# Linear attention with a cosine layer and soft experts: key maxima by VectorE and DRAM, token softmax on 128 columns

## The chip, the cores and the metric

The kernel runs on one core of one Trainium2 chip. The metric is the device time of one execution in microseconds. Engines are named as the profile names them: PE (TensorE), DVE (VectorE), ACT (ScalarE), POOL (GpSimd), SP (SyncE, which issues the DMAs).

## What is computed

```python
# q, k, v: 8 batches, 8 heads, 576 tokens, 64 wide
k_s = softmax(k, axis=tokens); q_s = softmax(q, axis=width)
x = q_s @ (k_s.T @ v)               # per batch and head; then 4608 tokens x 512
h = x @ w_in                         # 512 -> 2048
x = (h * cos(h)) @ w_out             # 2048 -> 512
logits = x @ phi                     # 32 slots: 8 experts of 4
d = softmax(logits, axis=tokens)     # over all 4608 tokens
slot_out = experts(d.T @ x)          # relu(s @ w1[e]) @ w2[e]
out = softmax(logits, axis=slots) @ slot_out
```

All inputs are float32 but for w_in and w_out, which come as 64-bit words and are narrowed on the chip.

## The kernel before

The tokens go through in ten parts: parts 0 to 7 have 512 tokens, parts 8 and 9 have 256. A part has 16 steps (one per 128 rows of the 2048-wide layer): `mm1` (line 917, twelve matmuls into a buffer of tag h, of which there are three), `round_u`, `frac`, `cosine` and `gate` (lines 922 to 941, on DVE and ACT), which make g = h cos h. Since only x @ phi and d.T @ x are needed of the second layer, phi is folded into w_out: `logits` (line 943) multiplies g by the folded wphi, several steps at a time (list NTL says after which steps), and `g_tr` (line 962) then transposes g in place on DVE in blocks of 32.

When a part's logits are complete (a 128x128 tile, 32 slots by four row groups of 128 tokens), `p1` copies them to LTs. `p2(d, 0)` spreads them with the constant rc to all row groups as 128 x 512 in PSUM (line 983). `p3` takes the running maximum, `p4` the exponent and sum, `p5` a block transposition into ee. `g_mm` (line 1035) accumulates ee.T @ g over tokens with 32 x 32 tiles, and `g_add` adds that to a total that `ac` rescales. `p2(d, 1)` and `c1` to `c3` make the slot softmax.

Keys are handled a batch ahead: `k_max` (line 632) reduces over the tokens that lie in one partition, `k_tr` transposes on PE (line 654), `k_diag` reduces (661) and multiplies with the identity (666), `k_bc` sums with ones to broadcast the maxima to all partitions (675), `k_bc_ev` copies them to km on ACT (681). Then `k_sub`, `k_exp`, `k_v`, `k_fin`. Queries: `q_max`, `q_sub`, `q_exp`, `q_sum`, `q_rec`, `q_mul`, transposition `q_tr` with its copy, `q_kv`, and the split of x into two halves `x_hi`, `x_lo`, from which `mm1` reads.

The order of the instructions on each engine is fixed when the kernel is built. `Issue` (line 257) is a list planner: each `op` has an engine, a cost, its predecessors and a due time from the table PLACES["AT"]; PLACES["ENG"] gives the engine where there is a choice (P is GpSimd, D VectorE, A ScalarE). Each engine then runs its queue strictly in order. PSUM buffers are counted in rings: four of tag m for everything around the main matmuls, three of tag h for `mm1`. All DMAs are issued by SP, also in order.

After the last part comes a tail: the totals are folded (`e_fold`), the expert weights (w_u, in units of 1 MB whose loads are released by buffers that come free) are multiplied in `e_si`, `e_w1`, `e_w2`, and `e_mm` writes the output. Where PE would stand, filler matmuls (`keep_warm`, line 1553) are queued.

## Time and profile before

| | before |
|---|---|
| time, median of 3 runs | 710.34 us (707.34 to 710.55) |
| the profiled execution, its own time | 714.83 us |
| its span, first to last instruction | 712.4 us |
| PE busy | 671.6 us, 94% |
| DVE busy | 566.7 us, 80% |
| ACT busy | 370.7 us, 52% |
| POOL busy | 117.2 us, 16% |
| PE's granted clock, mean | 0.967 |

A row of time gives the start from the beginning of the span, a duration, engine, line of the kernel, operation, output and inputs, shape and count. Records of pipelined matmuls overlap, so the distance from one start to the next tells what a matmul costs. A float32 matmul leaves two records.

### The profile page before, as it was taken

What the parts mean: (1) busy time and instruction counts of PE and PEld (TensorE: products, weight loads), DVE (VectorE), ACT (ScalarE), POOL (GpSimd) and SP (SyncE); (2) the same over time, 40 slices, a digit from 0 to 9 for tenths busy, and PEclk for the clock granted to TensorE, in tenths of its full rate; (3) what the DMA queues carried; (4) which work ended last, traced back from release to release, by engine and by line L of the source; (5) the groups of instructions that cost most, each with busy time, mean ns of one, the idle gap of its engine ahead of it and who ended that gap; (6) DMA issues with size and microseconds to landing.
All of it is one profiled execution on the core that took longest, in us unless ns stands there. A gap on an engine that the chain in (4) does not pass through costs nothing.

```text
span 712.4 us, 16382 instructions
## 1 busy us (share of the span) xinstructions
PE 671.6 (94%) x6901; PEld 494.4 (69%) x6901; DVE 566.7 (80%) x1077; ACT 370.7 (52%) x618; POOL 117.2 (16%) x116
## 2 busy tenths in 40 slices
PE   7599899999999999999999899999999999999991
PEld 5467676777777777787787578768778888853330
DVE  6779899898999999989998997886886887732142
ACT  2868887484465374477285745523553535410041
POOL 1433641320030150240232111000000000000000
PEclk9779899999999999999999999999999999999996
...
DMA packets 53032, 97.58 MB, mean 137 GB/s; under 512 B 7776, under 2 KB 33376, under 8 KB 47712
## 3 DMA queue, kind: packets, MB, share of 16 engines
...
q14 instruction: 18, 0.15, 0.1%
...
## 4 chain that ended last, share of the span: by engine, by line
PE 74%; DVE 11%; DMA 8%; ACT 2%; issue 1%; POOL 1%; SPq 1%; DVEq 0%; ACTq 0%; POOLq 0%
PE ps_h L917 48%; PE ps_m L1035 5%; PE ps_LT L957 4%; PE ps_LT L1553 3%; DMA w_u<-in_moe_w_dram 3%; PE ps_m L707 2%; DMA Q<-in_q_dram 2%; PE ps_m L566 2%; PE ps_m L607 2%; DMA KVB<-in_k_dram 2%; DVE T L933 2%; DVE G L964 1%; DMA out_dram<-ob 1%; PE ps_h L1224 1%; DVE G L941 1%
## 5 line engine op out<-in xcount | busy, mean ns | idle before, releaser
L917 PE MATMUL ps_h<-XH,W 128*128 128x512 f32 x1024 | 334.2, 399 | 1.0 <-DVE G L941 0.9
L917 PEld LDWEIGHTS ps_h<-XH,W 128*128 128x128 f32 x1024 | 192.8, 188 | 56.0 <-issue 10.5
L917 PE MATMUL ps_h<-XL,W 128*128 128x512 f32 x512 | 201.3, 393 | 0.0
L938 ACT ACTIVATE T<-T 128x512 f32<-128x512 f32 (+1 forms) x160 | 93.6, 590 | 139.8 <-DVE T L933 139.5
L941 DVE TENSOR_TENSOR G<-T,ps_h 128x512 f32<-128x512 f32 (+1 forms) x160 | 99.3, 627 | 24.7 <-ACT T L938 18.3
L933 DVE SCALAR_TENSOR_TENSOR T<-T,ps_h 128x512 f32<-128x512 int32 (+1 forms) x160 | 100.2, 628 | 16.8 <-ACT T L925 13.8
L917 PEld LDWEIGHTS ps_h<-XL,W 128*128 128x128 f32 x512 | 96.5, 189 | 20.1 <-DVE XL L630 0.4
L925 ACT ACTIVATE T<-ps_h,quarter 128x512 int32<-128x512 f32 (+1 forms) x107 | 68.7, 644 | 79.6 <-PE ps_h L917 78.2
L964 DVE STREAM_TRANSPOSE G<-G 128x512 f32<-128x512 f32 (+1 forms) x160 | 96.8, 636 | 0.8 <-PE ps_LT L957 0.8
L553 POOL TENSOR_TENSOR B<-Q,qm 128x512 f32<-128x512 f32 x23 | 26.4, 1155 | 200.4 <-PE ps_m L566 68.9
L917 PEld LDWEIGHTS ps_h<-xe,W 128*128 128x128 f32 x384 | 46.7, 188 | 2.7 <-DVE G L941 1.0
L917 PE MATMUL ps_h<-xe,W 128*128 128x256 f32 x384 | 48.5, 284 | 0.0
L1035 PE MATMUL ps_m<-G,A 32*32 32x512 f32 x1152 | 42.7, 620 | 0.9 <-DVE G L964 0.9
L531 POOL TENSOR_TENSOR Q<-Q,qm 128x512 f32<-128x512 f32 x26 | 28.2, 1089 | 89.1 <-DVE qm L528 87.0
L957 PE MATMUL ps_LT<-G,wphi 128*32 128x128 f32 x1152 | 39.3, 276 | 1.5 <-DVE G L941 1.4
L684 POOL TENSOR_TENSOR KVB<-KVB,km 128x576 f32<-128x576 f32 x24 | 35.9, 1525 | 18.6 <-ACT km L681 18.6
L957 PEld LDWEIGHTS ps_LT<-G,wphi 128*32 128x32 f32 x1152 | 29.4, 109 | 12.4 <-issue 9.0
L927 DVE TENSOR_SCALAR T<-ps_h 128x512 int32<-128x512 f32 (+1 forms) x53 | 33.3, 628 | 5.3 <-PE ps_h L917 5.2
L1553 PE MATMUL ps_LT<-ones 128*128 128x512 f32 x109 | 32.3, 442 | 2.1 <-DVE r L448 2.1
L938 ACT ACT_TABLE_LOAD x25 | 32.1, 1283 | 0.4
L1035 PEld LDWEIGHTS ps_m<-G,A 32*32 32x32 f32 x1152 | 19.5, 105 | 17.2 <-issue 9.2
L1553 PEld LDWEIGHTS ps_LT<-ones 128*128 128x128 f32 x109 | 21.8, 210 | 13.6 <-issue 7.4
...
## 6 DMA issues: line engine op xcount, KB each, us to landing
...
```

The source lines that it names most:

```text
L531: (nc.vector if eng == "DVE" else nc.gpsimd).tensor_tensor(out=qv(t), in0=qv(t), in1=qm[:, t].unsqueeze(2).to_broadcast([128, 8, 64]), op= ...
L684: (nc.vector if eng == "DVE" else nc.gpsimd).tensor_tensor(out=k_t[:, t], in0=k_t[:, t], in1=km[:, t].unsqueeze(1).to_broadcast([128, KC, ...
L917: nc.tensor.matmul(out=u_t[s], lhsT=w[:, wi, kk, o:o + 128], rhs=x[xi][:, kk], start=(kk == 0 and n == 0), stop=(kk == 3 and n == 2),)
L925: nc.scalar.activation(out=t.bitcast(I32), in_=u_t[s], func=ACTF.Identity, bias=quarter)
L927: nc.vector.tensor_scalar(out=t.bitcast(I32), in0=u_t[s], scalar1=0.25, scalar2=None, op0=ALU.add)
L933: nc.vector.scalar_tensor_tensor(out=t, in0=t.bitcast(I32), scalar=0.25, in1=u_t[s], op0=ALU.subtract, op1=ALU.subtract)
L938: nc.scalar.activation(out=t_t[s], in_=t_t[s], func=ACTF.Sin, scale=-UNDER_TWO_PI)
L941: nc.vector.tensor_tensor(out=g_of(s), in0=t_t.pop(s), in1=u_t.pop(s), op=ALU.mult)
L957: nc.tensor.matmul(out=lt_t[d][o:o + 32, 0:128], lhsT=w2sb[:, f], rhs=g[:, 128 * c:128 * c + 128], start=(f0 < m), stop=(f0 >= NF - m),)
L964: nc.vector.transpose(out=g_of(s), in_=g_of(s))
L1035: nc.tensor.matmul(out=st["gp"][i][32 * c:32 * c + 32].rearrange("p (f b) -> p f b", f=NF), lhsT=ee[o, 32 * j:32 * j + 32], rhs=gs(d)[o, : ...
L1553: nc.tensor.matmul(out=warm[when], lhsT=ones_r, rhs=ones_r.unsqueeze(1).to_broadcast([128, 4, 128]), start=True, stop=True,)
```

## The change

Three things change in what is computed where, and the planner's tables are new for nearly all operations.

- Token softmax of parts 0 to 7: `p2(d, 0)` is gone. The maximum, the exponent and the sum are taken on LTs itself, 128 columns, with a running maximum for each row group and slot. After a block transposition of 128 columns, `copies` spreads the result to all row groups by four matmuls of 32 rows with rr, one for each row group, into four buffers of tag m, and `take_copy` brings them to ee, on ACT or DVE. Before part 8, which works as before, `merge` brings the four row groups to one maximum.
- Keys of batches 2 to 7 (KROW): in place of `k_tr`, `k_diag`, `k_bc` and the copy there is `k_row`: DVE transposes km in blocks of 32 and reduces, a DMA writes the 128 x 8 maxima to DRAM, two DMAs read them back to 64 partitions each, and DVE takes the maximum of two halves into km.
- Loads: the first key loads are issued ahead of the first query loads.

Beside these, rr is made with the constants, `e_sel` stands earlier in the list, and part 0 takes its logits every two steps, part 9 in five groups in place of two. The diff without the due times and without the other engine strings:

```diff
...
-        "k_sub": "PPDDDPPPPDPDDPPPPPPPPDPPPPPPPPDP",
-        "q_sub": "PDDPPPPPPDPPPPPDDDDPPPPPPPDPPPPDPPDP",
-        "q_mul": "PDDPPDPPPPPPPDDPPDPDDPPPPDPDDPPPDPPD",
...
+        "k_sub": "DDPPPPPPPPPPPPPPPPDPPPDPDDPPPPPP",
+        "q_sub": "PDDPPPPPPPPPPPPPDPPPPPPPDPPDPPPPPPDD",
+        "q_mul": "DDDPPPPDDPPPPPPDPPPPPPPDPPDDPDDPPPPP",
...
+        "tc": "DAADAAADDDAAAADADAADDDADDADDAAAD",
...
-    "NTL": [[3, 7, 11, 15], [3, 7, 11, 15], [7, 15]],
+    "NTL": [[1, 3, 5, 7, 9, 11, 13, 15], [3, 7, 11, 15], [3, 7, 11, 13, 15]],
...
+    "KROW": 2,
...
         nc.vector.tensor_add(r32, r32, ident[:, 96:128])
+        nc.vector.tensor_copy(rr, r32.unsqueeze(1).to_broadcast([128, 4, 32]))
...
 
     km = sbt([128, 4, 64], "km1")
-    kmx = sbt([128, 4], "kmx")
+    kmx = sbt([128, 8], "kmx")
...
     def k_bc_ev():
         nc.scalar.copy(out=km.rearrange("p t d -> p (t d)"), in_=pm_t.pop("kb")[:, 0:256])
+    dram = ctx.enter_context(tc.tile_pool(name="dk", bufs=1, space=bass.MemoryType.DRAM))
+    kd = dram.tile([4, 256], F32, name="kd")
+    def k_row(part):
+        m = abuf[:, 3]
+        if part == 0:
+            nc.vector.transpose(out=m[:, 0:256], in_=km.rearrange("p t d -> p (t d)"))
+            nc.vector.reduce_max(
+                out=kmx, in_=m[:, 0:256].rearrange("p (j r) -> p j r", r=32), axis=AX.X
+            )
+        elif part == 1:
+            nc.sync.dma_start(out=kd.rearrange("g (e j) -> (g e) j", j=8), in_=kmx)
+        elif part == 2:
+            for h in range(2):
+                nc.sync.dma_start(
+                    out=m[64 * h:64 * h + 64],
+                    in_=kd[2 * h:2 * h + 2].rearrange("a f -> (a f)").partition_broadcast(64),
+                )
+        else:
+            nc.vector.tensor_tensor(
+                out=km.rearrange("p t d -> p (t d)").rearrange("p (j e) -> p j e", j=8),
+                in0=m[:, 0:256].rearrange("p (e j) -> p j e", j=8),
+                in1=m[:, 256:512].rearrange("p (e j) -> p j e", j=8), op=ALU.max,
+            )
     def k_sub(t, eng):
         (nc.vector if eng == "DVE" else nc.gpsimd).tensor_tensor(
...
     def p3(d):
-        nc.vector.reduce_max(out=es, in_=st["r"][:, 0:parts[d][2]], axis=AX.X)
+        if d < 8:
+            nc.vector.reduce_max(out=es, in_=st["lt"], axis=AX.X)
+        else:
+            nc.vector.reduce_max(out=es, in_=st["r"][:, 0:parts[d][2]], axis=AX.X)
         if d == 0:
             nc.vector.tensor_scalar(
                 out=nmx[0], in0=es, scalar1=-1.0, scalar2=None, op0=ALU.mult
             )
         else:
             nc.vector.scalar_tensor_tensor(
-                out=nmx[d % 2], in0=es, scalar=-1.0, in1=nmx[1 - d % 2], op0=ALU.mult, op1=ALU.min
+                out=nmx[d % 2], in0=es, scalar=-1.0,
+                in1=st.pop("nm")[:, 32:33] if d == 8 else nmx[1 - d % 2], op0=ALU.mult, op1=ALU.min
             )
     def p4(d):
-        nt = parts[d][2]
+        nt = 128 if d < 8 else parts[d][2]
         if d:
             nc.scalar.activation(
                 out=ac, in_=nmx[1 - d % 2], func=ACTF.Exp, scale=-1.0, bias=nmx[d % 2]
             )
         nc.scalar.activation(
-            out=eT[:, 0:nt], in_=st.pop("r")[:, 0:nt], func=ACTF.Exp, bias=nmx[d % 2],
-            accum_out=es if d else esacc,
+            out=eT[:, 0:nt], in_=st["lt"] if d < 8 else st.pop("r")[:, 0:nt], func=ACTF.Exp,
+            bias=nmx[d % 2], accum_out=es if d else esacc,
         )
     def p5(d):
-        nt = parts[d][2]
-        nc.vector.transpose(out=ee[:, 0:nt], in_=eT[:, 0:nt])
+        if d < 8:
+            nc.vector.transpose(out=eT[:, 128:256], in_=eT[:, 0:128])
+        else:
+            nt = parts[d][2]
+            nc.vector.transpose(out=ee[:, 0:nt], in_=eT[:, 0:nt])
+    def copies(d):
+        st["ex"] = [misc() for c in range(4)]
+        for c in range(4):
+            o = slice(32 * c, 32 * c + 32)
+            nc.tensor.matmul(
+                out=st["ex"][c][:, 0:128], lhsT=rr[o].rearrange("p r s -> p (r s)"),
+                rhs=eT[o, 128:256], start=True, stop=True, tile_position=(32 * c, 0),
+            )
+    def take_copy(d, c, eng):
+        (nc.vector.tensor_copy if eng == "DVE" else nc.scalar.copy)(
+            out=ee[:, 128 * c:128 * c + 128], in_=st["ex"][c][:, 0:128]
+        )
+    nm1 = sbt([128, 32], "nm1")
+    def merge(part):
+        if part == 0:
+            st["nm"] = misc()
+            nc.tensor.matmul(
+                out=st["nm"][0:1, 128:256], lhsT=nmx[1], rhs=ident, start=True, stop=True
+            )
+        elif part == 1:
+            nc.vector.tensor_reduce(
+                out=nm1[0:1], in_=st["nm"][0:1, 128:256].rearrange("p (c s) -> p s c", c=4),
+                axis=AX.X, op=ALU.min,
+            )
+        elif part == 2:
+            for n in range(4):
+                nc.tensor.matmul(
+                    out=st["nm"][32 * n:32 * n + 32, 32:33], lhsT=nm1[0:1], rhs=ones[0:1, 0:1],
+                    start=True, stop=True,
+                )
+        elif part == 3:
+            nc.vector.tensor_tensor(out=esacc, in0=esacc, in1=ac, op=ALU.mult)
+        elif part == 4:
+            st["em"] = misc()
+            nc.tensor.matmul(
+                out=st["em"][:, 0:1], lhsT=rr.rearrange("p r s -> p (r s)"), rhs=esacc,
+                start=True, stop=True,
+            )
     def p6(d):
+        if d == 8:
+            nc.vector.tensor_tensor(out=esacc, in0=st.pop("em")[:, 0:1], in1=es, op=ALU.add)
+            return
         nc.vector.scalar_tensor_tensor(
             out=esacc, in0=esacc, scalar=ac, in1=es, op0=ALU.mult, op1=ALU.add
         )
...
         for i in range(4):
             o = slice(32 * i, 32 * i + 32)
             for c in range(4):
-                j = 4 * jq + c
+                j = 4 * c + jq if d < 8 else 4 * jq + c
                 nc.tensor.matmul(
                     out=st["gp"][i][32 * c:32 * c + 32].rearrange("p (f b) -> p f b", f=NF),
                     lhsT=ee[o, 32 * j:32 * j + 32], rhs=gs(d)[o, :, 32 * j:32 * j + 32],
...
                 o, c0 = slice(32 * j, 32 * j + 32), 4 * (4 * eg + j)
                 nc.gpsimd.tensor_copy(out=sel[o, eg, c0:c0 + 4], in_=r32[o, c0:c0 + 4])
         nc.vector.reduce_sum(out=mask, in_=sel, axis=AX.X)
-        nc.vector.tensor_copy(rr, r32.unsqueeze(1).to_broadcast([128, 4, 32]))
     def e_pre():
...
             for part, cost in enumerate((0.6, 0.33, 0.2, 0.2)):
                 op(("k_max", b, tp, part), DVE, cost, k_max, b, tp, part, after=last, lock=True)
                 last = [("k_max", b, tp, part)]
-        op(("k_tr", b), PE, 0.45, k_tr, take="m",
-           after=[("k_max", b, 0, 3), ("k_max", b, 1, 3)])
-        op(("k_dg", b, 0), DVE, 0.35, k_diag, b, 0, give="m", after=[("k_tr", b)])
-        op(("k_dg", b, 1), DVE, 0.6, k_diag, b, 1, after=[("k_dg", b, 0)], lock=True)
-        op(("k_bc", b), PE, 0.6, k_bc, b, take="m", after=[("k_dg", b, 1)])
-        op(("k_bc_ev", b), ACT, 0.3, k_bc_ev, give="m", after=[("k_bc", b)])
+        done = [("k_max", b, 0, 3), ("k_max", b, 1, 3)]
+        if b < P["KROW"]:
+            op(("k_tr", b), PE, 0.45, k_tr, take="m", after=done)
+            op(("k_dg", b, 0), DVE, 0.35, k_diag, b, 0, give="m", after=[("k_tr", b)])
+            op(("k_dg", b, 1), DVE, 0.6, k_diag, b, 1, after=[("k_dg", b, 0)], lock=True)
+            op(("k_bc", b), PE, 0.6, k_bc, b, take="m", after=[("k_dg", b, 1)])
+            op(("k_bc_ev", b), ACT, 0.3, k_bc_ev, give="m", after=[("k_bc", b)])
+        else:
+            op(("k_row", b, 0), DVE, 0.75, k_row, 0, after=done)
+            op(("k_row", b, 1), DMA, 0.5, k_row, 1, more=1.9, slack=1.0, after=[("k_row", b, 0)])
+            op(("k_row", b, 2), DMA, 1.0, k_row, 2, more=1.9, data=True, after=[("k_row", b, 1)])
+            op(("k_bc_ev", b), DVE, 0.33, k_row, 3, lock=True, after=[("k_row", b, 2)])
         for t in range(4):
             op(("k_sub", b, t), None, 0, k_sub, t,
                after=[("k_bc_ev", b)], ways=[(POOL, 1.15, True, ()), (DVE, 0.7, True, ())])
...
                after=[("k_exp", b, (t,)) for t in ts] if first else [("k_exp", b, tuple(ts))])
             isu.ops["k_v", b, tp]["after"] += [("lv", b, t) for t in ts + [4]] + [("k_v", b, 0)] * tp
             isu.ops["k_v", b, tp]["after"] += [past("q_kv", b - 1, i) for i in range(2)]
-        op(("k_fin", b), DVE, 1.1, k_fin, b, give=("m", "m"), after=[("k_v", b, 1)])
+        op(("k_fin", b), DVE, 1.25, k_fin, b, give=("m", "m"), after=[("k_v", b, 1)])
     def q_ops(b):
         first = b == 0
         raw_x = [*hold("XH1"), *hold("XL1")] if b == 1 else []
         for t in range(4):
             op(("lq", b, t), DMA, 0.73, load_q, b, t, more=LATE,
-               after=[past("q_mul", b - 1, t)])
+               after=[past("q_mul", b - 1, t)] + [("lk", b, i) for i in range(2)] * first)
         for t in range(4):
             op(("q_max", b, t), DVE, 0.6, q_max, t, after=[("lq", b, t)])
             op(("q_sub", b, t), None, 0, q_sub, t, after=[("q_max", b, t)],
...
         nt = parts[d][2]
         k = nt // 128
         big = nt == 512
-        old = [past("p2", d - 1, 0), past("p2", d - 1, 1)]
+        old = [past("p2", d - 1, 0), past("p2", d - 1, 1), past("p4", d - 1)]
         op(("p1", d), ACT, 0.25, p1, d, after=[("tl", 16 * d + 15)] + old)
-        op(("p2", d, 0), PE, 0.215 * k, p2, d, 0, take="m", after=[("p1", d)])
+        if d >= 8:
+            op(("p2", d, 0), PE, 0.215 * k, p2, d, 0, take="m",
+               after=[("p1", d), ("g_mm", d - 1, parts[d - 1][2] // 128 - 1)])
         op(("p2", d, 1), PE, 0.12, p2, d, 1, take="m", after=[("p1", d)])
-        op(("p3", d), DVE, 0.8 if big else 0.5, p3, d,
-           after=[("p2", d, 0), past("p6", d - 1)])
-        op(("p4", d), ACT, 0.95 if big else 0.75, p4, d, table="exp", give="m",
-           after=[("p3", d), past("p5", d - 1), past("p6", d - 1)]
-           + [past("g_add", d - 1, i) for i in range(4)])
-        op(("p5", d), DVE, 0.7 if big else 0.4, p5, d,
-           after=[("p4", d), past("g_mm", d - 1, parts[d - 1][2] // 128 - 1) if d else None])
-        if d:
+        if d == 8:
+            op(("merge", 0), PE, 0.15, merge, 0, take="m",
+               after=[("p3", 7), ("g_mm", 7, 3)])
+            op(("merge", 1), DVE, 0.25, merge, 1, after=[("merge", 0)])
+            op(("merge", 2), PE, 0.15, merge, 2, after=[("merge", 1)])
+        free = [past("p5", d - 1), past("p6", d - 1)] + [past("g_add", d - 1, i) for i in range(4)]
+        if d < 8:
+            op(("p3", d), DVE, 0.42, p3, d, after=[("p1", d), past("p6", d - 1), past("p4", d - 1)])
+            op(("p4", d), ACT, 0.6 if d else 0.35, p4, d, table="exp", after=[("p3", d)] + free)
+            op(("p5", d), DVE, 0.25, p5, d, after=[("p4", d), past("copies", d - 1)])
+            op(("copies", d), PE, 0.3, copies, d, take="m", n_take=4,
+               after=[("p5", d), past("g_mm", d - 1, 3)])
+            for c in range(4):
+                op(("tc", d, c), None, 0, take_copy, d, c, give="m",
+                   after=[("copies", d), past("g_mm", d - 1, 3)],
+                   ways=[(ACT, 0.17, False, ()), (DVE, 0.2, False, ())])
+        else:
+            op(("p3", d), DVE, 0.5, p3, d, give="m" if d == 8 else (),
+               after=[("p2", d, 0), past("p6", d - 1)] + [("merge", 2)] * (d == 8))
+            op(("p4", d), ACT, 0.75, p4, d, table="exp", give="m",
+               after=[("p3", d), past("copies", d - 1)] + free)
+            op(("p5", d), DVE, 0.4, p5, d,
+               after=[("p4", d), past("g_mm", d - 1, parts[d - 1][2] // 128 - 1)])
+        if d == 8:
+            op(("merge", 3), DVE, 0.12, merge, 3, after=[("p4", d)])
+            op(("merge", 4), PE, 0.1, merge, 4, take="m", after=[("merge", 3)])
+            op(("p6", d), DVE, 0.12, p6, d, give="m", after=[("merge", 4)])
+        elif d:
             op(("p6", d), DVE, 0.12, p6, d, after=[("p4", d)])
         for jq in range(k):
             op(("g_mm", d, jq), PE, 1.08, g_mm, d, jq, take=None if jq else "m",
-               n_take=4, after=[("p5", d), ("g_mm", d, jq - 1) if jq else None]
+               n_take=4, after=[("g_mm", d, jq - 1) if jq else None]
+               + (each("tc", d) if d < 8 else [("p5", d)])
                + ([("tr", 16 * d + i) for i in range(NF)] if jq == 0 else []))
         for i in range(4):
             on_act = d == NB and i % 2 == 0
...
         if b > 1:
             post_ops(b - 2)
         q_ops(b)
+    op(("e_sel",), POOL, 2.0, e_sel, after=[("mm1", 48)], lock=True)
     S8, L, D = 16 * (NB - 1), 16 * NB, NB
     for s in range(S8, S8 + 16):
         step_ops(s)
...
     unit_ops(0, 23)
     for i in range(NFILL):
         op(("fill", i), PE, 0.22, keep_warm, 1, at=FILL, after=[("p1", D)])
-    op(("e_sel",), POOL, 2.0, e_sel, after=[("mm1", 48)], lock=True)
     op(("es",), DVE, 0.3, e_sum, after=[("p6", D)])
     op(("gT", 0), PE, 0.55, e_tr, 0, take="m", after=[("fold", 3)])
     op(("gT", 4), ACT, 0.48, e_tr, 4, give="m", after=[("gT", 0)])
```

## Rows read from the trace of the kernel before

**Rows 1.** The page, busy us, share of the span, instructions.
```profile
PE 671.6 (94%) x6901; PEld 494.4 (69%) x6901; DVE 566.7 (80%) x1077; ACT 370.7 (52%) x618; POOL 117.2 (16%) x116
```

**Rows 2.** Busy time by stretch: stretch, length, engines, granted clock, DMA share, GB/s.
```profile
0.00:120.00 120.00, 102.17 (x865) 74.36 (x865) 102.23 (x186) 86.86 (x147) 47.95 (x53) 0.89 0.81 262
120.00:620.00 500.00, 495.56 (x5276) 388.08 (x5280) 435.77 (x834) 267.64 (x440) 69.20 (x63) 1.00 0.23 72
620.00:712.40 92.40, 73.89 (x770) 31.91 (x760) 28.68 (x59) 16.25 (x33) 0.00 (x0) 0.91 0.80 325
```

**Rows 3.** Timeline of PE around `p2`, two parts: start, us, instruction.
```profile
138.03 1.05 PE L983 MATMUL ps_m<-LTs,rc 128*128 128x128 f32 x8
139.01 0.65 PE L675 MATMUL ps_m<-A,ones 128*64 128x256 f32 x4
139.60 0.50 PE L917 MATMUL ps_h<-XH,W 128*128 128x512 f32 x1
...
327.45 1.06 PE L983 MATMUL ps_m<-LTs,rc 128*128 128x128 f32 x8
328.27 0.48 PE L917 MATMUL ps_h<-XH,W 128*128 128x512 f32 x1
```

**Rows 4.** Timeline of PE, the transposition of the key maxima.
```profile
248.79 0.38 PE L654 MATMUL ps_m<-ident,km 128*128 128x128 f32 x2
249.10 1.96 PE L957 MATMUL ps_LT<-G,wphi 128*32 128x128 f32 x64
```

**Rows 5.** Timeline of PE, tiled groups and their neighbours.
```profile
142.02 0.39 PE L917 MATMUL ps_h<-XL,W 128*128 128x512 f32 x1
142.25 0.39 PE L917 MATMUL ps_h<-XH,W 128*128 128x512 f32 x1
142.56 1.08 PE L957 MATMUL ps_LT<-G,wphi 128*32 128x128 f32 x32
...
206.80 4.46 PE L1035 MATMUL ps_m<-G,A 32*32 32x512 f32 x128
211.19 0.50 PE L917 MATMUL ps_h<-XH,W 128*128 128x512 f32 x1
```

**Rows 6.** Groups by line and shape: busy us, mean ns, idle before.
```profile
L661 DVE TENSOR_REDUCE kmx<-ps_m 128x4 f32<-128x256 f32 x8 | 3.3, 414 | 0.0
L666 DVE TENSOR_TENSOR A<-ident,kmx 128x512 f32<-128x512 f32 x6 | 4.0, 668 | 0.0
L996 DVE TENSOR_REDUCE es<-ps_m 128x1 f32<-128x512 f32 x8 | 5.5, 682 | 0.8 <-PE ps_m L983 0.8
L1019 DVE STREAM_TRANSPOSE A<-A 128x512 f32<-128x512 f32 x8 | 5.6, 700 | 0.4 <-ACT A L1012 0.4
L1061 DVE TENSOR_REDUCE cm<-ps_m 128x4 f32<-128x128 f32 x8 | 2.2, 274 | 1.5 <-PE ps_m L989 1.5
L1080 DVE STREAM_TRANSPOSE cst<-cw 128x128 f32<-128x128 f32 x8 | 2.5, 311 | 0.3
```

**Rows 7.** By line, query loads, then writes to DRAM: issue to landing.
```profile
L507 SPq DMA_DIRECT2D Q<-in_q_dram x64: 311/426/1481, 0.7 to 396.1; - x64
DMA to landing us min/median/max: 2.0/3.0/11.7
...
L832 SPq DMA_DIRECT2D wo<-G x16: 319/376/1576, 39.7 to 112.6; - x16
DMA to landing us min/median/max: 2.0/3.7/9.8
```

**Rows 8.** Timeline of DVE, a wait for a query load: idle time before it in brackets.
```profile
384.49 0.69 DVE L528 TENSOR_REDUCE qm<-Q 128x8 f32<-128x512 f32 x1 [1.90 <-DMA Q<-in_q_dram]
```

**Rows 9.** The chain that ended last, its first DMA: start, us.
```profile
1.74 6.66 DMA KVB<-in_k_dram
```

**Rows 10.** Timeline of DVE and PE in the tail, part 9.
```profile
627.74 0.42 DVE L964 STREAM_TRANSPOSE G<-G 128x256 f32<-128x256 f32 x1
...
629.59 2.35 PE L1035 MATMUL ps_m<-G,A 32*32 32x512 f32 x64
```

More of the change, by code (lines that the diff above doesn't have):

```diff
@@ new lines @@
+        "q_sub": [-108.907, 90.961, -43.548, 301.155, -46.709, -78.856, -4.593, 327.301, 93.347,
[3 rows of a table added]
+        "q_exp": [13.497, 45.924, 25.572, -204.646, -43.836, -19.953, 180.847, 633.515, 392.045,
+            331.387, 409.287, 547.679],
+        "q_sum": [-236.664, -50.029, 275.663, 390.427, 90.29, 100.877, -112.416, 111.831, 68.788,
[3 rows of a table added]
+        "q_rec": [2.69, -52.652, 38.657, 114.664, 155.313, 295.471, 35.001, 313.136, 1105.602],
+        "q_mul": [-57.986, -25.832, -95.079, 134.382, 87.893, -24.657, 19.269, 109.887, 108.668,
[3 rows of a table added]
@@ new lines @@
+        "g_mm": [25.204, 46.22, 41.989, 175.435, -199.81, -231.64, -149.736, 80.369, 271.444,
[3 rows of a table added]
+        "g_add": [-187.104, -50.988, -181.958, -178.032, 183.494, 159.807, 300.386, 536.992, 271.63,
[11 rows of a table added]
+        "e_sel": [-4.675],
+        "merge": [569.706, 630.624, 646.329, 688.27, 796.046],
+        "pre": [813.24],
+        "fold": [932.96, 637.18, 560.078, 968.515],
[7 rows of a table added]
+        "siT": [222.942, 778.362, 955.398],
[13 rows of a table added]
+        "out": [960.535, 851.815, 690.843, 303.608, 811.941, 334.147, 428.943, 551.972, 382.592],
@@ L661, in k_diag @@
             nc.vector.reduce_max(
-                out=kmx,
+                out=kmx[:, 0:4],
                 in_=pm_t.pop("kT")[:, 0:256].rearrange("p (t h r) -> p h t r", t=2, h=2), axis=AX.X,
```

124 lines of the change are left out of this document (57 added, 67 removed), and 347 rows, old and new, of the table PLACES.

## The prediction

> **What bounds the kernel now.** I read the busy shares first [rows 1]: TensorE (PE) is busy 94% of the span and VectorE (DVE) 80%. An average says nothing of where, so the second view was busy time by stretch [rows 2]. It falls into three. From 0 to 120 us PE works 102.2 of 120 us: weights are loaded and converted, and no engine is alone the limit. From 120 to 620 us PE works 495.6 of 500 us at the full clock (1.00 granted), DVE 435.8. After 620 us PE works 73.9 of 92.4 us and the DMA engines 80%: weights of the experts stream in and the output goes out. In the middle stretch an instruction that leaves PE takes its whole time off the end, and one that leaves DVE does so only where DVE runs without a gap. The third view, PE's instructions in order of time, shows that this is no artefact of stretched records: in [rows 3, 5] each matmul starts where the one before it lets go. The reader should look at starts, not durations: a 128x512 matmul is recorded as 0.39 us, but the next one starts 0.23 us later [rows 5].
>
> **Token softmax of parts 0 to 7 on PE.** Before, four matmuls with rc (`p2`, part 0, line 983) spread the logits to all row groups. From their first start to the start of what follows is 0.98 us in one part and 0.82 us in another [rows 3]; I take 0.90. Eight parts: 7.2 us leave PE. In come `copies`: four matmuls of 32 rows by 128 columns. No such shape is in the trace. One bound is the expert accumulation (line 1035), 32-row matmuls of 512 columns: four groups of sixteen in 4.39 us [rows 5], so 1.10 us for 512 columns and 0.27 us for 128 if the four row groups work side by side as there. The other is 0.90 us if they run one after another as the rc matmuls do. I take 0.27, since line 1035 is the nearest shape. The matmul group that follows a full-size matmul in another tiling starts 0.31 us after it where the next full-size one starts after 0.23 [rows 5]: 0.08 us, and I charge it on either side, 0.16 in all. The Trainium skill (TensorEngine Tiling (Array Packing), Tiling Modes, Key Properties) says that a change of tiling mode drains TensorE; the rc matmuls ran in the mode of their neighbours, so this speaks against the change. By a drain the sum loses 8 x 0.16 = 1.3 us against none; the 0.08 us bears it out and the sum uses that. So copies cost 8 x 0.43 = 3.4 us, and PE gains 7.2 - 3.4 = **3.8 us** (bounds: 8 x (0.90 - 1.06) = -1.3, and 8 x (0.98 - 0.43) = +4.4).
>
> **Key maxima, batches 2 to 7.** Two transposes (line 654) hold PE 0.31 us [rows 4] and the broadcast with ones (line 675) 0.59 us, from 139.01 to 139.60 [rows 3]. Six batches: 6 x 0.90 = **5.4 us** leave PE. Nothing comes back to PE.
>
> **What is added to PE.** `merge` brings three sets of small matmuls, once. The nearest rows are 0.31 us for the pair of transposes and 0.59 for the broadcast; three sets are 0.9 to 1.8 us, and I take 0.9 as they are narrower than either. Logits are now taken every 2 steps in part 0 (four more groups) and in 5 groups instead of 2 in part 9 (three more): 7 x 0.16 = 1.1 us; part 0 partly lies where PE has idle time, so 0.8. PE's net: -3.8 - 5.4 + 0.9 + 0.8 = **-7.5 us**.
>
> **DVE.** A part's maximum goes from 512 columns to 128, 0.68 to 0.27 us, the transposition from 0.70 us to about a quarter of the columns, 0.31 [rows 6]: 8 x 0.80 = 6.4 us less. Of 32 copies out of PSUM the new table gives DVE 15, about 0.27 us each by the 128-column row: 4.1 us more; ScalarE's 17 lie in an engine that is busy 267.6 of the 500 us [rows 2]. Keys: 0.42 and 0.67 us go [rows 6], and a transposition, a reduction and a maximum of 256 columns come. I take 0.42 us for each by the 256-column reduction; 6 x (1.26 - 1.09) = 1.0 us more. The engine table hands 7 operations of 512 or 576 columns (2 `k_sub`, 3 `q_sub`, 2 `q_mul`) from DVE to GpSimd, 7 x 0.68 = 4.8 us less. Net -6.1 us. DVE's load falls about as fast as PE's, so it doesn't become the limit by itself where it has 64 us of idle time in 500 [rows 2]. The copy of rr (128 columns, so at most the 0.27 us) moves to the constants, in the shade of the first loads; `e_sel` is only listed earlier. Both count as nothing.
>
> **Start.** Keys first puts the two key loads where the first query loads stand. The chain that ends last begins with the first key load, issued at 1.74 us and landed at 8.40 [rows 9]. It can start about 1 us earlier and without 0.5 MB of queries ahead of it. DVE then has the query work and the key work together, so I take 1.0 us, bounds 0 and 2.2.
>
> **Tail.** Before, 16 transpositions of part 9 stand behind its last group of logits; they end at 628.16 and the accumulation starts at 629.59 [rows 10]. With 5 groups, 14 of 16 tiles are free earlier. That could give 3 us, but behind it the tail waits for weights (DMA engines 80% busy after 620 [rows 2]), so 1.0, bounds 0 and 3.
>
> **The wait that is added.** The key row goes to DRAM and back, and `k_bc_ev` on DVE waits for it. Behind that instruction DVE's queue holds the rounding, fraction and gate of the running steps; PE can go on for three steps (three buffers of tag h) and then stands. Both transfers go through SP, in order, behind query and value loads. A landing takes 2.0 us at best, 3.0 in the median and 11.7 at worst for query loads, and 2.0, 3.7 and 9.8 for writes to DRAM [rows 7]: 4.0, 6.7 and 21.5 us for both. The code's own due times allow 6.6 us (slack 1.0, costs 0.5 and 1.0, twice 1.9, and the hand-overs), so the median is nearly covered by other work. The one DVE wait of this kind in the middle stretch lasts 1.90 us [rows 8]. I take 1.0 us for all six, bounds 0 and 6 x 2.5 = 15.
>
> **Sum.** -7.5 - 1.0 - 1.0 + 1.0 = -8.5 us. The profiled execution took 714.83 us (span 712.40 and 2.43 around it), so 706.3 by its own time; it lies 4.5 us above the median of 710.34. From the median: 710.34 - 8.5 = **701.8 us**.
>
> **Rivals.**
> *More than the sum.* The shorter chains (logits to maximum without PE between) also close idle time; start and tail reach their bounds, 2.2 and 3 us, and nothing waits for the key row: -7.5 - 5.2 = -12.7, so 697.6. For it speaks that PE idles 17.8 us before 120 us; against it that the DMA engines are 81% busy there [rows 2].
> *DVE sets the pace.* The seven operations handed to GpSimd become late instead, DVE keeps only its own -1.3 us, and what leaves PE turns into idle time: -1.3 - 2.0 = -3.3, so 707.0, within the noise. DVE's 435.8 of 500 speaks against a bound on the average; in single stretches it has no gap. It decides where DVE would be over 99% busy, PE's own share, across the meeting of two parts.
> *The copies do not run side by side.* 8 x (0.90 + 0.16 - 0.90) = +1.3 instead of -3.8: 5.1 us less gain, 706.9. The 4.39 us of [rows 5] speaks against it.
> *The key row comes late (slower).* One mechanism: SP issues the write and the read behind query loads that wait for `q_mul`, the landing goes beyond 6.6 us, and DVE stands with the gates of the running steps behind it. From 8.5 / 6 = 1.4 us per batch of stall that reaches PE the whole gain is gone; at 2.5 us per batch it is 15 - 8.5 = +6.5, so 716.8. For it speaks the wait of [rows 8] behind loads issued just before; against it that the median round trip fits. The Trainium skill (DMA: Bandwidth & Descriptors, Anatomy of one DMA) says that a DMA's completion waits for a write receipt, with a "surprisingly long delay especially when the write target is HBM". The write median of 3.7 us against 3.0 for reads [rows 7] leans that way.
>
> **Chances.** Forecast 0.50, more than the sum 0.17, DVE 0.12, no overlap 0.08, late row 0.13. This kernel's measurement tells 0.5% (3.6 us) from no change. Faster by over that (below 706.8) is the forecast's share of 0.47, all of the second case and some of the borderline ones: 0.69. Slower (above 713.9) is most of the last: 0.12. The rest, 0.19, is the same. The range goes from a little under the second case, with the start and tail at their bounds and copies at theirs, 694, to 713, which leaves out the late row beyond 2 us per batch.
>
> **What would show it.** Right: PE in the middle stretch still above 98%, line 983 with 16 records instead of 80, lines 654 and 675 only for batches 0 and 1, the copies within 0.5 us from their first start to the next instruction, DVE waits for the key row under 1 us in sum. Wrong: DVE idle behind a landing of km or A several times for over 1 us, PE idle in the middle beyond 10 us, or copies of 0.9 us. A part 9 accumulation that starts no sooner after its last gate than before would strike the tail's term, a first mm1 at 39 us or later the start's.

## The result and the profile after

The changed kernel takes 689.24 us (median of 4 runs, 687.06 to 690.23) against 709.48 us in the runs made beside it; the ratio is 0.9714, 95% interval 0.9679 to 0.9749. It is 20.2 us faster where 8.5 us were forecast, and the time lies below the range of 694 to 713 us.

The page of after and its busy time by stretch, as in [rows 1, 2]:

```profile
PE 651.4 (95%) x6859; PEld 479.9 (70%) x6859; DVE 552.8 (80%) x1094; ACT 384.0 (56%) x642; POOL 120.0 (17%) x119
```
```profile
0.00:120.00 120.00, 107.88 (x939) 79.14 (x940) 111.22 (x212) 95.32 (x160) 49.42 (x52) 0.97 0.81 266
120.00:620.00 500.00, 493.98 (x5346) 382.93 (x5344) 423.56 (x858) 276.88 (x460) 70.61 (x68) 1.00 0.28 89
620.00:686.90 66.90, 49.51 (x577) 17.80 (x576) 18.03 (x25) 11.77 (x22) 0.00 (x0) 0.90 0.83 342
```

In the middle PE is as full as before. What has changed is the first stretch: in the first 120 us DVE works 111.2 us instead of 102.2, ACT 95.3 instead of 86.9, PE 107.9 instead of 102.2. The engines do more of their work early. How this adds up is seen from PE's timeline: the starts of the first `mm1`, of part 1's first `mm1` and of the last `mm1`, in us.

| kernel | first mm1 | part 1 | last mm1 | end of span |
|---|---|---|---|---|
| before | 39.2 | 120.8 | 618.4 | 712.4 |
| after | 34.0 | 108.4 | 599.0 | 686.9 |

Of the 25.5 us between these two spans, 12.4 are there when part 1 begins, 7.0 come in parts 1 to 9, 6.1 behind the last `mm1`. Before's profiled execution lies 5 us above its median; two variants of it below (e2, e4), with times like its median, have spans of 707.6 and 706.3. Part 1 begins at 121.8 and 118.4 there, part 1 to the last `mm1` takes 493.5 and 493.8 us, not 497.6, and 92.3 and 94.1 us are left behind it. Against their mean after gains 20.1 us: 11.7 before part 1, 3.1 in parts 1 to 9 (490.6 in after, 488.6 to 491.6 in the variants of after that leave these parts alone) and 5.3 behind. These are the better figures.

### The profile page after: what moved, and what is told of

Same layout as the page of the kernel before. It is cut to its first block, busy times and chain, and to the rows that moved or that the text cites. A ratio compares the mean times of both kernels' runs of the same rounds, so it can differ in the third digit from the quotient of the medians.

```text
span 686.9 us, 16358 instructions
## 1 busy us (share of the span) xinstructions
PE 651.4 (95%) x6859; PEld 479.9 (70%) x6859; DVE 552.8 (80%) x1094; ACT 384.0 (56%) x642; POOL 120.0 (17%) x119
## 4 chain that ended last, share of the span: by engine, by line
PE 68%; DVE 11%; DMA 10%; ACT 6%; issue 2%; SPq 1%; POOL 0%; DVEq 0%; ACTq 0%
PE ps_h L1001 45%; PE ps_m L1173 6%; PE ps_LT L1041 4%; DMA w_u<-in_moe_w_dram 3%; DMA Q<-in_q_dram 2%; PE ps_m L624 2%; PE ps_m L665 2%; PE ps_m L791 2%; DVE T L1017 2%; PE ps_LT L1719 2%; DMA out_dram<-ob 1%; DVE G L1025 1%; DMA KVB<-in_v_dram 1%; DVE G L1048 1%; DMA rwo<-in_moe_w_out_dram 1%
## 5 line engine op out<-in xcount | busy, mean ns | idle before, releaser
L1025 DVE TENSOR_TENSOR G<-T,ps_h 128x512 f32<-128x512 f32 (+1 forms) x160 | 99.2, 626 | 25.5 <-ACT T L1022 15.8
L611 POOL TENSOR_TENSOR B<-Q,qm 128x512 f32<-128x512 f32 x25 | 28.8, 1165 | 183.9 <-PE ps_m L624 66.1
L589 POOL TENSOR_TENSOR Q<-Q,qm 128x512 f32<-128x512 f32 x29 | 31.4, 1089 | 101.9 <-DVE qm L586 101.9
L1041 PE MATMUL ps_LT<-G,wphi 128*32 128x128 f32 x1152 | 41.0, 276 | 1.0 <-DVE G L1025 1.0
L1041 PEld LDWEIGHTS ps_LT<-G,wphi 128*32 128x32 f32 x1152 | 29.4, 109 | 11.2 <-issue 6.7
L1173 PEld LDWEIGHTS ps_m<-G,A 32*32 32x32 f32 x1152 | 19.7, 103 | 15.5 <-issue 8.6
L1719 PE MATMUL ps_LT<-ones 128*128 128x512 f32 x91 | 27.8, 446 | 2.1 <-DVE r L505 2.1
L1719 PEld LDWEIGHTS ps_LT<-ones 128*128 128x128 f32 x91 | 18.1, 211 | 12.6 <-issue 7.1
## 6 DMA issues: line engine op xcount, KB each, us to landing
rwi<-in_moe_w_in_dram SPq DMA_DIRECT2D x7, 1024.0 KB, 11.2
```

The costliest lines, as they stand in the source:

```text
L589: (nc.vector if eng == "DVE" else nc.gpsimd).tensor_tensor(out=qv(t), in0=qv(t), in1=qm[:, t].unsqueeze(2).to_broadcast([128, 8, 64]), op= ...
L1025: nc.vector.tensor_tensor(out=g_of(s), in0=t_t.pop(s), in1=u_t.pop(s), op=ALU.mult)
L1041: nc.tensor.matmul(out=lt_t[d][o:o + 32, 0:128], lhsT=w2sb[:, f], rhs=g[:, 128 * c:128 * c + 128], start=(f0 < m), stop=(f0 >= NF - m),)
L1173: nc.tensor.matmul(out=st["gp"][i][32 * c:32 * c + 32].rearrange("p (f b) -> p f b", f=NF), lhsT=ee[o, 32 * j:32 * j + 32], rhs=gs(d)[o, : ...
L1719: nc.tensor.matmul(out=warm[when], lhsT=ones_r, rhs=ones_r.unsqueeze(1).to_broadcast([128, 4, 128]), start=True, stop=True,)
```

## The experiments

A load is named as `lk` (k), `lq`, `lv` (v; `lv4` is the one of 64 columns), `wi`, `wo` (pieces of w_in and w_out). Changes are against after's 689.2 us, for kernels made from before against its 709.6 us (708.8 for e9).

### The start

**e1, old load order.** The first loads of after in before's order:
```diff
-lk1 lk0 lq2 lq1 lq0 lq3 wo0 lv0 lv4 wi0 phi lv3 lv1 lv2
+lq3 lq1 lk0 lk1 lv1 lq2 lq0 lv4 lv0 lv3 wi0 lv2 phi wo0
```


> The changed kernel with only the first fourteen loads put back in the order of the kernel before (q 3, q 1, both k, v 1, q 2, q 0, the 64-column v load, v 0, v 3, the first w_in piece, v 2, phi, the first w_out piece); every engine's order and all arithmetic stay those of the changed kernel. Theory L (the order of the first loads on SP's queue, above all the weights that now pass ahead of the wait for v 1, makes the 12.4 us by which part 1 starts sooner): the time goes up by 7 to 12 us, first mm1 near 39 us, part 1 starts at 115 to 121 us. Theory E (the planned order on ACT and DVE makes it, the loads don't matter): up by less than 2 us, part 1 at 108 to 110 us. Theory P (the chunk-wise logits of part 0 make it): less than 2 us too.


Measured: 696.84 us, +7.6 (ratio to before 0.9818, 0.9786 to 0.9849); first `mm1` 43.3, part 1 at 117.2. The loads matter.

**e2, new load order on before**, the reverse edit on the kernel before.


> The kernel before with only its first fourteen loads in the order of the changed kernel (both k, q 2, q 1, q 0, q 3, first w_out piece, v 0, the 64-column v load, first w_in piece, phi, v 3, v 1, v 2); its engine orders stay. Theory L: the first weights are there some 9 us sooner, but its DVE begins with q 3, which now comes sixth, so a part is lost: 3 to 8 us less, part 1 starting at 113 to 118 us instead of 120.8. Theory E: no gain or a loss of 1 to 4 us, since DVE and ACT stand at q 3 and the conversions keep their places behind it.


Measured: 710.29 us (ratio 1.0008, 0.9988 to 1.0029); part 1 at 121.8. The same order of loads gives nothing under the old engine orders. Neither theory had the two results together.

**e3, weights late** (after) and **e4, weights early** (before):
```diff
-lk1 lk0 lq2 lq1 lq0 lq3 wo0 lv0 lv4 wi0
+lk1 lk0 lq2 lq1 lq0 lq3 lv1 lv4 wo0 lv0 wi0
...
-lq3 lq1 lk0 lk1 lv1 lq2 lq0 lv4 lv0 lv3 wi0 lv2 phi wo0
+lq3 lq1 lk0 lk1 lv1 lq2 lq0 wo0 wi0 lv4 lv0 lv3 lv2 phi
```


> The changed kernel with v 1 and the 64-column v load issued ahead of the first weights, so that SP waits for v 1's landing before the weights, as in the kernel before; k stays ahead of q. Theory L: first weight piece issued near 10.5 us instead of 4.4, time up by 4 to 8 us, part 1 starting at 112 to 117 us. Theory K (k ahead of q makes the gain at the start): 0 to 1 us. Theory E: 0 to 2 us.

> The kernel before with the first w_out and w_in pieces issued ahead of the 64-column v load, so ahead of SP's wait for v 1; nothing else. Theory L: weights issued near 5 us instead of 13.5 and 15.2, time down by 4 to 9 us, part 1 starting at 112 to 117 us instead of 120.8. Theory K: 0 to 1 us. Theory E: within 1.5 us, since the conversions stand at the same places of ACT's and DVE's orders.


Measured: e3 690.49 us, +1.3 (0.9733, 0.9699 to 0.9767), part 1 at 110.5; e4 709.93 us (1.0007, 0.9985 to 1.0029), part 1 at 118.4. Theory L, as it stood, falls.

**e5, q first** (after): two query loads back ahead of the keys.
```diff
-lk1 lk0 lq2 lq1
+lq2 lq1 lk1 lk0
```


> The changed kernel with q 2 and q 1 issued ahead of both k loads, as the kernel before has two q loads first; all else of the changed kernel stays, the early weights too. Theory K (with the engine orders of the changed kernel, whose DVE begins with the key maxima, the start hangs on k's landing): up by 4 to 7 us, the rest of the 7.6 us of the old load order once the 1.3 us of late weights are taken off; first mm1 at 38 to 42 us. Theory V (the old order cost by where v 1, v 0 and v 3 stand): up by less than 2 us.


Measured: 691.12 us, +1.9 with overlapping intervals (0.9736, 0.9702 to 0.977); first `mm1` 34.7, part 1 at 109.1. Theory K falls: that k comes ahead of q is worth 0.7 us at part 1 in the trace, and at most some 2 us in the time.

**e11, first weights last** (after):
```diff
-lk1 lk0 lq2 lq1 lq0 lq3 wo0 lv0 lv4 wi0 phi lv3 lv1 lv2
+lk1 lk0 lq2 lq1 lq0 lq3 lv1 lv4 lv0 lv3 wi0 lv2 phi wo0
```


> The changed kernel with both k and all q loads first as they are, and then v 1, the 64-column v load, v 0, v 3, the first w_in piece, v 2, phi, and the first w_out piece last, so that this piece is issued some 11 us later, as in the run with the old load order. Theory W (beyond a slack of some 5 us each us of the weights' delay delays the whole first part; the old order cost 7.6 us through the weights, not through k): up by 5 to 8 us, part 1 at 114 to 117 us. Theory KW (old order's cost needs k behind q and the weights late together): up by 1 to 3 us.


Measured: 696.22 us, +7.0 (0.9825, 0.9805 to 0.9845); first `mm1` 42.1, part 1 at 115.9. Theory W stands: this is e1's loss with k and q left in front. ACT's timeline shows how: the first conversion of w_out (`G<-rwo`) in after, e3 and e11, idle time in brackets, and behind it in e11 the copy of the key row:

```profile
12.47 0.67 ACT L858 ACTIVATE G<-rwo 128x512 f32<-128x512 f32 x1
```
```profile
16.10 0.66 ACT L864 ACTIVATE G<-rwo 128x512 f32<-128x512 f32 x1 [3.92 <-DMA rwo<-in_moe_w_out_dram]
```
```profile
22.74 0.66 ACT L864 ACTIVATE G<-rwo 128x512 f32<-128x512 f32 x1 [10.49 <-DMA rwo<-in_moe_w_out_dram]
23.30 0.36 ACT L745 COPY km<-ps_m 128x256 f32<-128x256 f32 x1
```

A queue that runs strictly in order holds the key row, and all that follows from it, behind a weight that isn't there. The wait of 10.5 us moves the first `mm1` by 8.1 us; the 1.5 us behind the wait of 3.9 lie within the spread of such starts (last section). In the kernel before, ACT's queue waits first for other things. Its timeline, SP's timeline of before, SP's waits there (us in total, times, longest), and SP's timeline of after:

```profile
14.63 0.63 ACT L538 ACTIVATE Q<-Q 128x512 f32<-128x512 f32 x1 [7.85 <-POOL Q L531]
17.28 0.37 ACT L681 COPY km<-ps_m 128x256 f32<-128x256 f32 x1 [2.02 <-PE ps_m L675]
...
19.82 0.66 ACT L774 ACTIVATE A<-rwi 128x512 f32<-128x512 f32 x1 [1.64 <-DMA rwi<-in_moe_w_in_dram]
```
```profile
3.27 1.54 SPq L507 DMA_DIRECT2D Q<-in_q_dram  x2
10.71 0.37 SPq L499 DMA_DIRECT2D KVB<-in_v_dram  x1
11.13 2.35 SPq L494 DMA_DIRECT2D KVB<-in_v_dram  x2
13.52 0.51 SPq L748 DMA_DIRECT2D rwi<-in_moe_w_in_dram  x1
```
```profile
SPq L499 <- DMA KVB<-in_v_dram: 15.3, 3, 5.9
```
```profile
1.75 2.61 SPq L565 DMA_DIRECT2D Q<-in_q_dram  x4
4.39 0.47 SPq L839 DMA_DIRECT2D rwo<-in_moe_w_out_dram  x1
```

Before, SP stands from 4.8 to 10.7 us, the 5.9 us in which `lv4` (line 499) waits for an earlier v load to land, and the first weight is issued at 13.5 us; but ACT's queue has it behind queries for which it stands 7.85 us and waits only 1.64 us for the weight itself. So e4, which takes SP's stand away from the weights, brings part 1 forward by 2.4 us in its profile (118.4 against 120.8) and gains nothing in the time: the loads have to agree with the places that the plan gave to their users.

**e9, new order on before**, and **e10, old order on after**: the first 535 operations, loads and engines' choice included, in the other kernel's order; what is computed stays each kernel's own.
```diff
-order = plan(own due times)
+order = first(535, plan of the other) + rest(own plan)
```


> The kernel before with all its own operations, but the first 535 of them (those that the changed kernel's plan starts in its first 110 us, up to the second chunk of part 1) issued in the changed kernel's order, on the engines chosen there, loads included; logits of part 0 stay in groups of four, p2 and the key transposes stay. Theory O (the order of the first 110 us, loads and engines together, makes the 11.5 us at the start): part 1 starts at 108 to 113 us instead of about 120, time down by 7 to 11 us. Theory P (the operations themselves, above all the finer logits groups of part 0, make it): down by 0 to 3 us.

> The reverse: the changed kernel with its own operations, the first 535 of them in the order, and on the engines, of the kernel before (loads included). Theory O: part 1 starts at 117 to 122 us instead of about 109, time up by 8 to 12 us. Theory P: up by 0 to 3 us.


Measured: e9 700.52 us, -8.3 (0.991, 0.9879 to 0.9941), part 1 at 113.1. With no operation changed, the order with its choice of engines gives 8.3 us by the medians and 6.4 by the ratio (4.2 to 8.6); the seven executions of e9 scatter from 698.9 to 707.7, and the profiled one is the slowest. e10: part 1 at 117.1, 8.7 us later than in after, as theory O has it. Its whole time is 709.60 us, +20.4 where 8 to 12 were expected: part 1 takes 78.1 us instead of 66.2 where the two orders are joined, and what of that belongs to the order isn't shown. DVE's share shows the mechanism. Stretches 0 to 60 and 60 to 120 us of before, the first of e9, both of after, the first of e1 and of e11 (columns as in [rows 2]; DVE is the third busy time, the granted clock stands behind POOL's):

```profile
0.00:60.00 60.00, 47.21 (x323) 33.33 (x324) 45.41 (x85) 36.02 (x61) 22.38 (x32) 0.83 0.96 311
60.00:120.00 60.00, 54.97 (x543) 41.04 (x542) 56.82 (x102) 50.83 (x86) 25.57 (x22) 0.94 0.66 213
```
```profile
0.00:60.00 60.00, 46.69 (x378) 33.88 (x379) 51.58 (x99) 41.03 (x69) 23.94 (x31) 0.94 1.02 343
```
```profile
0.00:60.00 60.00, 50.20 (x389) 36.87 (x389) 53.72 (x107) 44.29 (x75) 24.11 (x31) 0.94 1.03 345
60.00:120.00 60.00, 57.68 (x550) 42.27 (x551) 57.50 (x106) 51.03 (x86) 25.31 (x21) 1.00 0.59 187
```
```profile
0.00:60.00 60.00, 42.72 (x337) 31.18 (x338) 45.20 (x90) 35.48 (x61) 21.95 (x29) 0.89 0.87 300
```
```profile
0.00:60.00 60.00, 41.05 (x342) 30.31 (x343) 46.41 (x92) 36.65 (x63) 22.01 (x29) 0.89 0.90 308
```

From 60 to 120 us DVE has little room (56.8 and 57.5 of 60). In the first 60 us of before it idles 14.6 us; in after 6.3, in e9 8.4. e1 and e11, which differ from after in the order of loads alone, idle 14.8 and 13.6 us there, 8.5 and 7.3 more than after; their part 1 starts 8.8 and 7.5 us later, and their times are 7.6 and 7.0 longer. Between kernels of the same operations and engine orders, DVE's idle time ahead of a stretch that DVE nearly fills comes off the end nearly whole. In the kernel before, e4 idles 3.4 us less (11.2), and the time shows none of it.

One rival stays untested here, TensorE's clock. The stretches 32 to 36 and 36 to 44 us of before, 36 to 44 of after, 32 to 36 of e6, a variant that has after's start:

```profile
32.00:36.00 4.00, 1.31 (x9) 0.92 (x12) 4.00 (x8) 3.46 (x7) 1.06 (x1) 0.77 1.07 301
36.00:44.00 8.00, 7.24 (x33) 3.99 (x26) 4.61 (x9) 3.37 (x7) 4.08 (x4) 0.50 1.08 302
```
```profile
36.00:44.00 8.00, 7.71 (x35) 6.09 (x36) 7.96 (x13) 6.50 (x11) 5.15 (x5) 1.00 1.03 398
```
```profile
32.00:36.00 4.00, 4.00 (x22) 1.25 (x21) 2.59 (x5) 1.53 (x4) 0.55 (x1) 0.50 1.02 277
```

In before PE works 1.31 of the 4 us from 32 on, and for the next 8 us the granted clock is 0.50, the lower of its two levels; PE is then busy 7.24 of 8 us and DVE idles 3.4. In after the clock is 1.00 there, and DVE idles 0.04; e6 meets 0.50 from 32 to 36 us, and DVE idles 1.4 of 4. So a few of DVE's 14.6 us go with the clock, and what the order gives through it and what beside it no run separates. In e1 and e11 the clock is 1.00 from 36 to 44 us, so their loss doesn't come from these 8 us.

**e7, coarse logits of part 0** (after):
```diff
-"NTL": [[1, 3, 5, 7, 9, 11, 13, 15], ...
+"NTL": [[3, 7, 11, 15], ...
```


> The changed kernel with the logits of part 0 in four groups of four chunks, as before, instead of eight groups of two; six of its transposes then come later in DVE's order, behind their group. Theory P (the finer groups make part 0 shorter, since DVE gets transposes to do between conversions): up by 3 to 7 us, part 0 (34.0 to 108.4 us) longer by as much. Theory O (the planned order of part 0's conversions on ACT and DVE does it): up by less than 1.5 us.


Measured: 691.51 us, +2.3 (0.9741, 0.9718 to 0.9764, which overlaps with after's interval); part 0 takes 75.9 us instead of 74.4, where the variants with after's part 0 have 73.7 to 77.0. Between the theories; a small share, not settled by the time alone.

**e14, v load in four** (after):
```diff
-dma(v_t[:, :, 517:581], src[:, :, 512:576])
+for i in range(4): dma(v_t[:, i, 517:581], src[:, i, 512:576])
```


> The changed kernel with the 64-column v load of every batch cut into four loads, one for each head pair, so that no load of v overlaps another and SP does not wait for one to land before it issues the next. Theory W (the first weights were already ahead of the wait, and the rest has slack): within 1.5 us. Theory Q (the queue's wait still delays what DVE needs in the first 60 us): down by 2 to 5 us.


Measured: 688.54 us, -0.7 (0.9697, 0.9661 to 0.9734), within what the runs can tell: SP's remaining wait has slack.

### The middle

**e8, expansions back** (after): behind the copies, into columns that nobody reads.
```diff
+for c in range(4):
+    matmul(out=ex[c][:, 128:256], lhsT=rc[:, c], rhs=eT[:, 0:128])
```


> The changed kernel with the four logit expansions of each of the parts 0 to 7 put back on TensorE as additional matmuls of the same shape (their result is not used), next to the four copies. Theory E (TensorE sets the pace of the middle): up by 8 x 0.90 = 7.2 us, 6 to 8. Theory D (DVE or ACT sets it): up by less than 2 us.


Measured: 695.42 us, +6.2 (0.9797, 0.9773 to 0.9821). TensorE sets the pace here. In six of the eight parts the next matmul group starts 1.52 us after the copies instead of 0.43, 1.09 more. In parts 2 and 7 PE stands behind the copies already in after (0.70 and 1.47 us, for DVE), and the put-back matmuls add 0.15 and 0.33: 7.0 us in all on PE's timeline. Part 0 in e8, the copies and the expansions behind them:

```profile
127.88 0.50 PE L1123 MATMUL ps_m<-A,rr 32*128 32x128 f32 x8
128.31 1.16 PE L1128 MATMUL ps_m<-A,rc 128*128 128x128 f32 x8
129.40 1.08 PE L1047 MATMUL ps_LT<-G,wphi 128*32 128x128 f32 x32
```

**e12, key transposes back** (after), ahead of `k_v` of batches 2 to 7:
```diff
+for h in range(2): transpose(kvp[h][:, 136:264], km[:, 2 * h:2 * h + 2], ident)
+for h in range(2): matmul(kvp[0][64 * h:64 * h + 64, 264:512], ones[:, 0:64], km[:, 0:248])
```


> The changed kernel with the two 128x128 transposes and the two ones-broadcast matmuls (248 columns instead of 256) of the batches 2 to 7 put back on TensorE as additional work whose result is not used, right ahead of that batch's key-value products. Theory E (TensorE sets the pace): up by 6 x 0.90 = 5.4 us at most, 4 to 6, less than in the kernel before where they also stood behind DVE. Theory D: up by less than 1.5 us.


Measured: 692.37 us, +3.1 (0.9773, 0.975 to 0.9797): below theory E's 4 to 6, above D's 1.5. The matmuls put back do take PE's time; in e12, then in after (XH, W is `mm1`, KVB `k_v`):

```profile
139.12 0.39 PE L1016 MATMUL ps_h<-XH,W 128*128 128x512 f32 x1
139.35 0.38 PE L791 MATMUL ps_m<-ident,km 128*128 128x128 f32 x2
139.66 0.64 PE L795 MATMUL ps_m<-km,ones 128*64 128x248 f32 x4
140.23 1.28 PE L806 MATMUL ps_m<-KVB 64*64 64x66 f32 x72
```
```profile
137.30 0.39 PE L1001 MATMUL ps_h<-XH,W 128*128 128x512 f32 x1
137.62 1.28 PE L791 MATMUL ps_m<-KVB 64*64 64x66 f32 x72
```

From the last `mm1` start to that of `k_v` it is 1.11 us here and 0.32 in after, and the difference of 0.79 is the same in all six batches: 4.7 us in all. Why the time shows 3.1 of them is open.

**e13, copies twice** (after):
```diff
+for c in range(4):
+    matmul(out=ex[c][:, 128:256], lhsT=rr[32c:32c+32], rhs=eT[32c:32c+32, 128:256], tile_position=(32c, 0))
```


> The changed kernel with the four 32-row copies of each of the parts 0 to 7 issued twice, the second set into columns that nobody reads. Theory A (side by side on the four row groups, 0.43 us a set of four to the next start, as the profile of the changed kernel has it): up by about 8 x 0.43 = 3.4 us, less if only the first set pays for the change of tile form: 1.5 to 4. Theory B (one after the other, as four full matmuls): 8 x 0.9 = 7 us.


Measured: 688.85 us, -0.4 (0.9707, 0.967 to 0.9744). Theory B is excluded, A's size is below what the time can tell; PE's timeline can. In after, then in e13, the copies (`A,rr`, eight records for four matmuls) from one start to the next:

```profile
128.29 0.39 PE L1001 MATMUL ps_h<-XL,W 128*128 128x512 f32 x1
128.52 0.39 PE L1001 MATMUL ps_h<-XH,W 128*128 128x512 f32 x1
128.84 0.50 PE L1117 MATMUL ps_m<-A,rr 32*128 32x128 f32 x8
129.27 1.08 PE L1041 MATMUL ps_LT<-G,wphi 128*32 128x128 f32 x32
```
```profile
128.31 0.50 PE L1123 MATMUL ps_m<-A,rr 32*128 32x128 f32 x8
128.64 0.40 PE L1129 MATMUL ps_m<-A,rr 32*128 32x128 f32 x8
128.97 1.08 PE L1047 MATMUL ps_LT<-G,wphi 128*32 128x128 f32 x32
```

One set takes 0.43 us to the next start, two sets 0.66: the second adds 0.23 us. The first also starts 0.32 us after the matmul ahead of it, where the next full one starts after 0.23 (128.29 to 128.52 in the same timeline). So four copies cost 0.23 us and the two changes of tile form 0.09 and 0.20, 0.29 together. The logits group behind them has a tile form of its own: in [rows 5] it starts 0.31 us after a full-size matmul that it follows at once. So a part's copies add 0.32 + 0.43 - 0.31 = 0.44 us to PE.

### The tail

**e6, last logits in two groups** (after):
```diff
-"NTL": [..., [3, 7, 11, 13, 15]]
+"NTL": [..., [7, 15]]
```


> The changed kernel with the logits of the last part in two groups of eight chunks, as before, instead of five groups. Theory T (the transposes of the last part stand behind the last logits group: eight of them after a group of eight, two after a group of two): the first routing matmul of the last part moves from 7.1 to about 11.2 us after the last mm1, time up by 3.5 to 4.5 us. Theory S (the forecast's sum): up by 1.0 us. Theory N (the tail waits for expert weights anyway): up by less than 0.5 us.


Measured: 692.50 us, +3.3 (0.975, 0.9725 to 0.9774). The last transposes on DVE and the routing matmuls on PE, after and e6; the last `mm1` is at 598.96 and 600.07 us:

```profile
604.55 0.43 DVE L1048 STREAM_TRANSPOSE G<-G 128x256 f32<-128x256 f32 x1
...
606.03 2.35 PE L1173 MATMUL ps_m<-G,A 32*32 32x512 f32 x64
```
```profile
605.74 0.76 DVE L1050 STREAM_TRANSPOSE G<-G 128x256 f32<-128x256 f32 x2
...
607.36 0.76 DVE L1050 STREAM_TRANSPOSE G<-G 128x256 f32<-128x256 f32 x2
...
609.09 0.40 DVE L1050 STREAM_TRANSPOSE G<-G 128x256 f32<-128x256 f32 x1
...
610.58 2.35 PE L1175 MATMUL ps_m<-G,A 32*32 32x512 f32 x64
```

With two groups, transposes still stand between the softmax's operations, the last at 609.09, and the routing begins 10.5 us after the last `mm1`; with five it begins after 7.1, in before [rows 10] after 11.2. What follows does not swallow it: `e_w1` begins 15.1 us behind the routing's first matmul in all three.

**e15, a last group of one** (after):
```diff
-"NTL": [..., [3, 7, 11, 13, 15]]
+"NTL": [..., [3, 7, 11, 13, 14, 15]]
```


> The changed kernel with the last logits group of the last part cut once more, so that one chunk instead of two stands behind it. Theory T (a transpose of 0.63 us less and one logits matmul group less behind the last mm1): down by 0.6 to 1.0 us in the trace, the first routing matmul at 6.3 to 6.6 us after the last mm1 instead of 7.1. Theory S (something else ends last there already, the sums of the softmax): no change.


Measured: 688.30 us, -0.9 (0.9702, 0.9668 to 0.9737), no difference; the routing still begins at 7.1 us. Theory S: PE now waits for the softmax's own transposition on DVE. The gain was used up by the change.

## Why the prediction was wrong

**The middle was right in its mechanism and taken somewhat too large.** PE bounds it, as [rows 2, 3] said: the expansions put back on PE come back in the time (6.2 of 7.0 us), the key matmuls in part (3.1 of 4.7). The forecast took 7.2 us for the expansions. It took 0.43 us a part for the copies, as 0.27 for the matmuls and 0.16 for the change of form; PE's timeline has 0.23 and, net, 0.21, 0.44 together or 3.5 us for eight parts. The keys were taken at 5.4 us; whether the missing part of their 4.7 lies within the spread of the runs is open. The spans give 3.1 us for the middle, the put-back runs less the copies 6.2 + 3.1 - 3.5 = 5.8 with the merge not counted; the forecast's terms there (PE -7.5, key row +1.0) made 6.5.

**The key row and DVE.** Forecast 1.0 us of waits, measured 1.2, once, a little over the 1 us that the prediction named as its sign. The landings of the row's transfers, over all six batches, and DVE's groups by line (as in [rows 6]): the end of the key chain with its wait, the copies out of PSUM, the transposition of 128 columns:

```profile
DMA to landing us min/median/max: 1.4/2.9/3.9
```
```profile
L761 DVE TENSOR_TENSOR km<-A 128x256 f32<-128x256 f32 x6 | 4.0, 659 | 1.3 <-DMA A<-kd 1.2
L1123 DVE COPY A<-ps_m 128x128 f32<-128x128 f32 x15 | 3.7, 283 | 3.0 <-PE ps_m L1117 3.0
L1107 DVE STREAM_TRANSPOSE A<-A 128x128 f32<-128x128 f32 x8 | 2.4, 300 | 0.4 <-ACT A L1100 0.3
```

The median of 2.9 us lies under half of the 6.7 assumed for both legs, and the maximum far under the 11.7 of [rows 7]. The copies (283 ns against 0.27 us) and the transposition (300 against 0.31) came as forecast, the maximum of line 761 (659 against 0.42) did not. The late row didn't come; its worst case, 15 - 8.5, counted the 1.0 us of waits twice and should have been +5.5. Nor did DVE set the pace: it is busy 423.6 of 500 us, and 97.0% at most in the 20 us around the meeting of two parts, where that rival asked for 99%.

**The step that failed is Start.** It priced one thing, the first key load of the chain [rows 9], at 1.0 us with bounds 0 and 2.2. The order of the first 110 us, for which it had no term, gives 8.3 us by the medians and 6.4 by the ratio (e9); the finer logits of part 0 may give 2.3 more, which isn't clear of the noise (e7). Keys ahead of queries, the only thing weighed there, is worth between nothing and 2 us (e5); 7.0 us hang on the place of the first weights ahead of v loads in SP's queue (e11), which the diff's due times for `lwo` and `lv` decide, together with conversions that ACT has early enough to use them. The forecast read in [rows 2] that PE works 102.2 of the first 120 us, beside DVE's 102.2, and concluded that no engine is alone the limit. Split at 60 us the same view says otherwise: 14.6 us idle, then 56.8 of 60. The upper bound of the start's term was DVE's idle time ahead of the full stretch, 14.6 us, not 2.2. Nor did it have a term for the clock, which [rows 2] give as 0.89 in this stretch and after's view as 0.97.

**Tail.** The mechanism was named and the size was wrong: 1.0 us, because the tail waits for weights, against 3.3 (e6) and 4.1 in the profile. The weights end the tail later, but the chain from the routing to `e_w1` keeps its length, so a routing that starts sooner ends sooner. Its upper bound of 3 was near; the discount was not read from any row.

**The sum in parts:** order 8.3 (6.4), logits of part 0 2.3, expansions 6.2, keys 3.1, copies -3.5, tail 3.3: 19.7 (17.8) of 20.2 us. The agreement is closer than its terms are known: the copies are taken from PE's timeline, the 2.3 may be noise. The merge and the additional logits groups were not tried one by one. The rival "more than the sum" pointed the right way with a ceiling taken from the same narrow bounds.
